# Weight conversions held back to the 40th exponential, the first MLP's share of TensorE started eleven steps late instead of four, and eight PSUM copies moved to ScalarE

## The chip, the cores and the metric

The kernel runs on one core of one Trainium2 chip. The metric is the device time of one execution in microseconds. The time before is the median of three runs, 1116.79 us.

## The reference

The kernel computes three things in a row: an attention with rotary embedding over 4 batches, 8 heads, 576 positions and a head dimension of 64; a first MLP on the 2304 resulting tokens (512 to 2048 to 512), with a piecewise quadratic between its two layers; a second MLP of the same sizes with a squared relu.

```python
def _attn_ref(q, k, v):                       # each (4, 8, 576, 64)
    ...
    q_rot, k_rot = (rotate(q), rotate(k))
    scores = scale * np.matmul(q_rot, k_rot.transpose(0, 1, 3, 2))
    scores = scores - np.max(scores, axis=-1, keepdims=True)
    attn = np.exp(scores)
    attn = attn / (np.sum(attn, axis=-1, keepdims=True) + 1e-09)
    return np.matmul(attn, v).astype(np.float32)

def _moe_ref(x, w_in, w_out):                 # x: (2304, 512)
    h = x @ w_in
    ...
    g = np.where(pos, h, np.where(neg, 0.0, (h + beta) ** 2 / (4.0 * beta)))
    return (g @ w_out).astype(np.float32)

def _moe2_ref(x, w_in, w_out, s, b):
    h = x @ w_in
    r = np.maximum(h, 0.0)
    g = s * (r * r) + b
    return (g @ w_out).astype(np.float32)
```

The MLP weights come as 64-bit floats. Products are made in a reduced 32-bit format on TensorE with each operand split into a high and a low part, so one product is three matmuls (high by high, high by low, low by high).

## The kernel before

**Attention in units.** Two heads make a pair, and there are 16 pairs: four for each batch. A pair is nine units: four blocks of 128 queries for each of its two heads, and one unit for the two heads' last 64 queries together. So there are 144 units, counted from 0, and units 0 to 35 are the first batch. One unit is: scores on TensorE (`sc`, L357), the row maximum on VectorE (`nm`, L359), the exponential on ScalarE (`p`, L364; the list `exps` keeps these instructions, so `exps[n]` is unit n's), four transposes on TensorE (`tp`, L379), a copy of them out of PSUM on ScalarE (L382, L384) or VectorE (L386), and the product with v (`av`, L405). Twice in a pair `trem` transposes what remains of each row, the last 128 columns (`tr`, L392 and L395), and copies it to `ptr` (L397). GpSimd multiplies the next pair's q and k with the rotary table in between (L96 on `qin`, `kin`).

**Weight conversions.** A 128 by 512 block of 64-bit weights is converted in one go: a copy on ScalarE (L134), four bit operations on VectorE (L135 to L138), a rounding copy on ScalarE (L139), then a subtraction and an addition on GpSimd, each in two pieces (L96, tiles `wm` and `w`). Scratch tiles `wa` and `wm` exist once, so conversions follow one another. 24 of them lie inside the attention: 16 blocks of the first MLP's first half (`convert`), and 8 that are written back to memory (`park`).

**The first MLP beside the attention.** When a batch's attention is done, a generator `beside` with that batch's tokens is put on the list `fill`. It is asked for a step some 0.62 times per unit up to unit 76 and 0.92 times later; a step is one block of 12 matmuls (`h` or `y`, L181). Ahead of its first block it yields `LEAD` empty steps. What remains of the list after the last unit is run at the end of the attention. Three such lists come in: 16, 48 and 16 blocks, 960 matmuls together.

**What sets the order.** Up to the end of the attention a list scheduler places each instruction on its engine, by priorities in the order of the code. `tc.issue_after(x)` adds the condition that an instruction isn't issued before x. So `exps[n - 14]` at a conversion is what holds it back. After the attention TensorE's order is that of the code.

Of the kernel before, what the change touches and what calls it, by code (L numbers as in the profile page):

```python
# [24 lines left out]
NP = H // 2  # L25
# [11 lines left out]
RB = 2  # L37
XB = 3
N2 = 464
LEAD = 4  # L40
LT = 2
LA = 4
PB = 3
# [23 lines left out]
def kernel(ctx, tc, qq, kk, vv, tab, ww1, ww2, s, b, out):  # L67
    nc = tc.nc
# [44 lines left out]
    exps, tps, maxs = {}, {}, {}  # L113

    class Slice:
# [6 lines left out]
        def convert(self, raw, pools, hi, lo):  # L122
            if not wide:
                split(hi, lo, raw, nc.scalar, nc.gpsimd)
                return


            top = raw.bitcast(F32).rearrange("p (n t) -> p n t", t=2)[:, :, 1]
            low = raw.bitcast(U16).rearrange("p (n t) -> p n t", t=4)[:, :, 1]
            pool = pools[self.f * 2 + self.made & 1 if len(pools) > 1 else 0]  # L130
            a = pool.tile([P, HW], F32, tag="wa", name="wa", bufs=WB)
            m = pool.tile([P, HW], F32, tag="wm", name="wm", bufs=WB)
            au, mu = a.bitcast(U32), m.bitcast(U32)
            nc.scalar.activation(a, top, AF.Copy, scale=2.0 ** -112)  # L134
            nc.vector.tensor_scalar(out=mu, in0=au, scalar1=3, scalar2=None, op0=ALU.logical_shift_left)  # L135
            nc.vector.scalar_tensor_tensor(out=mu, in0=au, scalar=0x80000000, in1=mu, op0=ALU.bitwise_and, op1=ALU.bitwise_or)
            nc.vector.tensor_scalar(out=au, in0=mu, scalar1=0xFF800000, scalar2=None, op0=ALU.bitwise_and)
            nc.vector.scalar_tensor_tensor(out=a, in0=low, scalar=2.0 ** -36, in1=a, op0=ALU.mult, op1=ALU.mult)  # L138
            nc.scalar.copy(hi, m)  # L139
            pool_tt(out=m, in0=m, in1=hi, op=ALU.subtract)  # L140
            pool_tt(out=lo, in0=m, in1=a, op=ALU.add)
# [108 lines left out]
    def bank(name):  # L250
        return ps_b.tile([P, 512], F32, tag="bank", name=name)
# [6 lines left out]
    def load_qk(i, nm, pieces=WHOLE):  # L258
        bb, hp = divmod(i, NP)
        t = att2.tile([P, 2, S], F32, tag="qkin", name=f"{nm}in", bufs=QB)  # L260
        for c in pieces:
            nc.sync.dma_start(out=t[:, :, c], in_=(qq if nm == "q" else kk)[bb, hp, :, :, c])
        qk_in[nm, i] = t

    def load_v(i):
        bb, hp = divmod(i, NP)
        t = att2.tile([P, 5, 2, D], F32, tag="vin", name="vin", bufs=VB)
        for out, src in ((t[:, :, 1], vv[bb, hp, :, :, 1]), (t[:D, :4, 0], vv[bb, hp, D:, :4, 0]), (t[D:, :4, 0], vv[bb, hp, :D, 1:, 0]), (t[D:, 4, 0], vv[bb, hp, :D, 0, 0])):
            nc.sync.dma_start(out=out, in_=src)
        v_in[i] = t  # L270
# [15 lines left out]
    def rope_pair(i, nm, mul, add, lo_eng, pieces=WHOLE):  # L286

        t = qk_in[nm, i]
        tt = {nc.gpsimd: pool_tt, nc.vector: nc.vector.tensor_tensor}
        last = None  # L290
        for c in pieces:
            tt[mul](out=t[:, :, c], in0=t[:, :, c], in1=tab_sb[:, :, c], op=ALU.mult)
            r = t[:, 1, c]
            tt[add](out=r, in0=t[:, 0, c], in1=r, op=ALU.add)
            last = (lay_q if nm == "q" else lay_k)(i, t, c, lo_eng)
        return last
# [4 lines left out]
    def lay_q(i, t, c, lo_eng, heads=range(2)):  # L301

        st = stacks["q", i] = qs_t[i % 2]
        r = t[:, 1, c]
        for j in heads:
            own, other = SELF[j], SELF[1 - j]
            at = slice(j * QW + c.start, j * QW + c.stop)
            h = nc.scalar.activation(st[own, at], r[own], AF.Copy, scale=0.125)
            m = nc.vector.scalar_tensor_tensor(out=st[other, at], in0=r[own], scalar=0.125, in1=st[own, at], op0=ALU.mult, op1=ALU.subtract)
        return h.ins, m.ins  # L310
# [30 lines left out]
    pt = {}  # L341
# [46 lines left out]
    def trem(i, g):  # L388

        tp = bank("tr")  # L390
        for n in range(2):
            nc.tensor.transpose(tp[:, n * P:(n + 1) * P], p_t.pop((i, 2 * g + n))[:, 512:640], ident)  # L392
        m = 256
        if g == 0:
            nc.tensor.transpose(tp[:, 256:384], p_t.pop((i, 4))[:, 512:640], ident)  # L395
            m = 384
        nc.vector.tensor_copy(pt["r", g][:, :m], tp[:, :m])  # L397

    def av(i, g, ps, kts):

# [63 lines left out]
    def split_x(c, again):  # L464
        xh = m1.tile([P, KD, N1], F32R, tag="xh", name="xh")
        xl = m1.tile([P, KD, N1], F32R, tag="xl", name="xl")
        if again:
            return load_parts((xh, xl), c * N1, N1)
        for k in range(KD):
            xs = m2.tile([P, N1], F32, tag="xs", name="xs", bufs=3)  # L470
            nc.sync.dma_start(out=xs, in_=xd[k, :, c * N1:(c + 1) * N1])
            split(xh[:, k, :], xl[:, k, :], xs, nc.scalar, nc.gpsimd)
        return xh, xl
# [3 lines left out]
    def beside(work):  # L477
        x = split_x(work[0][0], work[0][0] in kept)
        for _ in range(LEAD):
            yield 1.0  # L480
# [48 lines left out]
    def turned_by(t, c):  # L529
        nc.vector.tensor_tensor(out=t[:, :, c], in0=t[:, :, c], in1=tab_sb[:, :, c], op=ALU.mult)  # L530
        return nc.vector.tensor_tensor(out=t[:, 1, c], in0=t[:, 0, c], in1=t[:, 1, c], op=ALU.add).ins
# [53 lines left out]
    def do_load(n):  # L585
        if n == 0:
            with tc.issue_after(turned):
                turned_by(tq, QP[1])
                lay_q(0, tq, QP[1], None)
        elif n in (1, 2):  # L590
            with tc.issue_after(maxs[n]):
                if n == 1:
                    turned_by(tq, QP[2])
                else:
                    lay_q(0, tq, QP[2], None)
        if n < len(units):
            i, k = units[n]
            if i + 1 < NPAIR:
                if i == 0 and k in (2, 6):
                    with tc.issue_after(maxs[k]):  # L600
                        turned_by(qk_in["q", 1], HALVES[k // 6])
                if i == 0 and k in (4, 5, 7, 8):
                    with tc.issue_after(maxs[k]), tc.issue_after(exps[k - 1]):
                        lay_q(1, qk_in["q", 1], HALVES[k // 6], None, [int(k in (5, 8))])
                if i and k == 0:
                    with ExitStack() if i > 1 else tc.issue_after(parts[1][1]), ExitStack() if i > 1 else tc.issue_after(maxs[9]):
                        rope_pair(i + 1, "q", nc.gpsimd, nc.vector, None)
                elif k == 2:
                    with ExitStack() if i else tc.issue_after(exps[2]), ExitStack() if i else tc.issue_after(lowest):
                        rope_pair(i + 1, "k", nc.gpsimd, nc.gpsimd, [nc.gpsimd, nc.vector])  # L610
                elif k == 7:
                    load_v(i + 1)
                elif k in (4, 6) and i + 2 < NPAIR:
                    load_qk(i + 2, "q" if k == 4 else "k")

        if n in range(33, 51, 2) or n in range(70, 110, 4):
            with tc.issue_after(exps[n - 14]):
                convert()

        if n in PARK_AT and parking:  # L620
            with tc.issue_after(exps[n - 4]):
                parking.pop(0).park(wst, scratch)()

    def do_t(n):
        if LT <= n < len(units) + LT:
            i, k = units[n - LT]
            tmain(i, k)
            if k in (4, 8):
                trem(i, k // 8)
                rbs[i, k // 8] = inverse(i, k // 8)  # L630
# [23 lines left out]
    def do_fill(n):  # L654
        if n < 48:
            return
        with tc.issue_after(exps[min(n, len(units)) - 4]):
            run_fill(0.62 if n < 76 else 0.92)

    acts = {"q": do_qk, "l": do_load, "t": do_t, "a": do_av, "f": do_fill}  # L660
    for n in range(len(units) + LA):
        with ExitStack() as st:
# [541 lines left out]
```

## Time and profile before

| | us |
|---|---|
| three runs: median (lowest to highest) | 1116.79 (1115.44 to 1121.0) |
| profiled execution, its own time | 1116.36 |
| its span from the first to the last instruction | 1114.6 |
| TensorE matmul busy | 1071.6 (96%) |
| VectorE busy | 783.8 (70%) |
| ScalarE busy | 626.7 (56%) |
| GpSimd busy | 428.6 (38%) |

Busy time is the union of an engine's instruction times. TensorE's matmuls overlap one another in the records, so its busy time is not the time that its work needs. The granted clock was 0.999 over the span.

### The profile page before, as it was taken

To read this page: it belongs to the slowest core of one execution; us is meant where nothing else is said; L and a number is where in the kernel's file an instruction comes from. 1 tells how busy PE (TensorE), PEld (TensorE's weight loads), DVE (VectorE), ACT (ScalarE), POOL (GpSimd) and SP (SyncE) were. 2 spreads that over 40 slices of the span, in tenths; PEclk is the share of its full clock that TensorE was granted. 3 is DMA by queue.
4 is the path that set the end of the run, shared out by engine and by line. 5 is a ranking of instruction groups with operands and counts; after the bars stand their busy time and mean duration, and the time that the engine had idled before them with its cause. 6 is when DMAs were issued, how large, how long until landed. Compare 5 with 4: busy or idle time off the path is not lost.

```text
span 1114.6 us, 20055 instructions
## 1 busy us (share of the span) xinstructions
PE 1071.6 (96%) x7296; PEld 979.2 (88%) x7296; DVE 783.8 (70%) x1453; ACT 626.7 (56%) x1432; POOL 428.6 (38%) x564
## 2 busy tenths in 40 slices
PE   5898999999999999999999999999999999999998
PEld 4666787778888889999999999999999999999997
DVE  7989998887666663454657666867777778677754
ACT  5777877767656665454545445474555448334431
POOL 6988978785553332332544445110212110000000
PEclk9999999999999999999999999999999999999999
DMA  8665956665656544656465663231322843221220
GB/s 240 170 190 163 270 162 212 216 191 152 213 179 189 173 151 140 223 167 194 146 187 204 211 228 113 94 113 59 116 87 90 303 169 117 83 82 44 81 63 36
DMA packets 109762, 173.24 MB, mean 155 GB/s; under 512 B 29408, under 2 KB 80608, under 8 KB 109664
## 3 DMA queue, kind: packets, MB, share of 16 engines
q1 hardware_dynamic: 109664, 171.97, 49.0%
q8 instruction: 57, 0.93, 0.4%
q14 instruction: 41, 0.34, 0.1%
HBM read 110.10 MB, written 48.56 MB: 142 GB/s over the span
## 4 chain that ended last, share of the span: by engine, by line
PE 73%; DVE 8%; POOL 7%; DMA 6%; ACT 3%; issue 3%; SPq 0%; POOLq 0%; DVEq 0%; ACTq 0%
PE hps L181 14%; PE sum L940 14%; PE yps L856 6%; PE yps L854 6%; PE yps L855 6%; PE yps L790 4%; PE yps L791 4%; PE yps L792 4%; PE h L181 3%; PE sc L357 3%; PE y L181 3%; PE av L405 3%; POOL kin L96 3%; PE tp L379 2%; DVE nm L359 2%
## 5 line engine op out<-in xcount | busy, mean ns | idle before, releaser
L181 PE MATMUL hps<-xh,w 128*128 128x288 f32 (+4 forms) x640 | 163.4, 325 | 0.0
L364 ACT ACTIVATE p<-sc,nm 128x576 f32<-128x576 f32 x144 | 106.5, 741 | 40.6 <-DVE nm L359 35.7
L357 PE MATMUL sc<-kh,qs 128*128 128x288 f32 x336 | 102.6, 328 | 25.6 <-ACT p L364 14.8
L359 DVE TENSOR_REDUCE nm<-sc 128x1 f32<-128x576 f32 x144 | 106.8, 748 | 20.5 <-PE sc L357 19.8
L948 ACT ACTIVATE four<-four,b_sb,s_sb 128x480 f32<-128x480 f32 x64 | 47.4, 782 | 127.8 <-DVE four L947 127.8
L856 PE MATMUL yps<-gh,w 128*128 128x480 f32 (+1 forms) x320 | 118.6, 371 | 0.0
L854 PE MATMUL yps<-gh,w 128*128 128x480 f32 (+1 forms) x320 | 118.5, 370 | 0.0
L855 PE MATMUL yps<-gl,w 128*128 128x480 f32 (+1 forms) x320 | 118.5, 370 | 0.0
L181 PEld LDWEIGHTS hps<-xh,w 128*128 128x128 f32 x640 | 113.3, 188 | 1.0
L96 POOL TENSOR_TENSOR wm<-wm,w 128x256 f32<-128x256 f32 x80 | 67.8, 867 | 109.2 <-ACT w L139 62.3
L181 PE MATMUL hps<-xl,w 128*128 128x288 f32 (+4 forms) x320 | 103.7, 324 | 0.0
L357 PEld LDWEIGHTS sc<-kh,qs 128*128 128x128 f32 x336 | 63.3, 191 | 45.2 <-ACT p L364 26.3
L790 PE MATMUL yps<-gh,w 128*128 128x288 f32 (+3 forms) x288 | 93.2, 323 | 1.2 <-DVE yp L797 0.7
L357 PE MATMUL sc<-kz,qs 128*128 128x288 f32 x336 | 92.9, 299 | 0.0
L792 PE MATMUL yps<-gh,w 128*128 128x288 f32 (+3 forms) x288 | 92.9, 323 | 0.0
L791 PE MATMUL yps<-gl,w 128*128 128x288 f32 (+3 forms) x288 | 92.9, 323 | 0.0
L379 PE MATMUL tp<-ident,p 128*128 128x128 f32 x576 | 87.3, 276 | 2.6 <-DVE pt L386 1.8
L96 POOL TENSOR_TENSOR wm<-wm,raw 128x256 f32<-128x256 f32 x16 | 12.8, 820 | 175.1 <-ACT raw L139 175.1
L405 PE MATMUL av<-pt,vin 128*64 128x256 f32 (+1 forms) x512 | 75.1, 418 | 1.3 <-ACT pt L382 0.8
L181 PE MATMUL y<-gh,w 128*128 128x288 f32 x320 | 73.9, 303 | 1.4 <-ACT pt L382 0.4
L379 PEld LDWEIGHTS tp<-ident,p 128*128 128x128 f32 x576 | 70.1, 142 | 5.6 <-DVE pt L386 2.8
L181 PE MATMUL h<-xh,w 128*128 128x288 f32 x320 | 71.8, 301 | 2.9 <-DVE pt L386 2.1
(153 smaller groups left out, 2888.5 us busy)
## 6 DMA issues: line engine op xcount, KB each, us to landing
wraw<-in_ww SPq DMA_DIRECT2D x56, 512.0 KB, 4.2
w<-parkd SPq DMA_DIRECT2D x24, 512.0 KB, 6.1
kin<-in_k SPq DMA_DIRECT2D x15, 576.0 KB, 5.6
qin<-in_q SPq DMA_DIRECT2D x15, 576.0 KB, 5.1
kh<-kin SPq DMA_DIRECT2D x60, 144.0 KB, 3.1
parkd<-wraw SPq DMA_DIRECT2D x16, 512.0 KB, 3.2
xs<-y1d SPq DMA_DIRECT2D x32, 240.0 KB, 2.7
xd<-u SPq DMA_DIRECT2D x16, 288.0 KB, 2.6
```

The lines of the kernel that those rows point to most:

```text
L96: m = nc.gpsimd.tensor_tensor(out=out[c], in0=in0[c], in1=in1[c], op=op)
L181: m = nc.tensor.matmul(out_ps, l, r, start=(i == 0), stop=(i == n - 1))
L357: nc.tensor.matmul(sc[:, half, o:o + n], l, r[:, k0:k0 + n], start=m == 0, stop=m == len(todo) - 1)
L359: maxs[i * 9 + k] = nc.vector.tensor_reduce(out=nm, in_=sc[:, :, :288], axis=AX.XY, op=ALU.max, negate=True).ins
L379: m = nc.tensor.transpose(v[:, c, :], p[:, c * P:(c + 1) * P], ident)
L790: nc.tensor.matmul(acc, wh, gh, start=f == 0, stop=False)
L791: nc.tensor.matmul(acc, wh, gl, start=False, stop=False)
L792: nc.tensor.matmul(acc, wl, gh, start=False, stop=last)
L854: nc.tensor.matmul(acc, wh, gh, start=f == 0, stop=False)
L855: nc.tensor.matmul(acc, wh, gl, start=False, stop=False)
L856: nc.tensor.matmul(acc, wl, gh, start=False, stop=last)
L940: nc.tensor.matmul(acc, l, r, start=j == 0, stop=j == len(t) - 1)
```

## The change

`LEAD` goes from 4 to 11. The first nine conversions are placed at units 45 to 61 (every second) instead of 33 to 49, and held behind `exps[n - 5]` (units 40 to 56) instead of `exps[n - 14]` (units 19 to 35). In the four pairs of the first batch (`i < NP`) the copy L397 is made by ScalarE instead of VectorE.

```diff
-LEAD = 4
+LEAD = 11
...
-        nc.vector.tensor_copy(pt["r", g][:, :m], tp[:, :m])
+        (nc.scalar.copy if i < NP else nc.vector.tensor_copy)(pt["r", g][:, :m], tp[:, :m])
...
-        if n in range(33, 51, 2) or n in range(70, 110, 4):
-            with tc.issue_after(exps[n - 14]):
+        if n in range(45, 63, 2) or n in range(70, 110, 4):
+            with tc.issue_after(exps[n - 5 if n < 63 else n - 14]):
                 convert()
```

VectorE's row around units 19 to 22, before. `nm` is the maximum of a unit, `pt` and `ptr` are copies out of PSUM, `wm` and `wa` belong to a conversion, `u` is the attention's result.

```order
L386 COPY pt<-tp 128x4x128
L397 COPY ptr<-tr 128x256
L135 TENSOR_SCALAR wm<-wa 128x512
L359 TENSOR_REDUCE nm<-sc 128x1
L136 SCALAR_TENSOR_TENSOR wm<-wa,wm 128x512
L359 TENSOR_REDUCE nm<-sc 128x1
L441 TENSOR_TENSOR u<-av,r 128x256
L443 TENSOR_TENSOR u<-av,r 64x64
L444 TENSOR_TENSOR u<-av,r 64x64
L137 TENSOR_SCALAR wa<-wm 128x512
L386 COPY pt<-tp 128x4x128
L138 SCALAR_TENSOR_TENSOR wa<-wraw,wa 128x512
```

The same place in the changed kernel:

```order
L386 COPY pt<-tp 128x4x128
L359 TENSOR_REDUCE nm<-sc 128x1
L441 TENSOR_TENSOR u<-av,r 128x256
L443 TENSOR_TENSOR u<-av,r 64x64
L444 TENSOR_TENSOR u<-av,r 64x64
L359 TENSOR_REDUCE nm<-sc 128x1
L386 COPY pt<-tp 128x4x128
```

The conversion's four instructions and the copy of `tr` are gone from between the maxima. In ScalarE's row the copy L397 now stands behind an L382 or between two exponentials, and the 24 conversions begin behind exponentials number 41, 45, 51, 57, 62, 67, 70, 75, 79, 81, 85, 88, 90, 96, 100, 106, 108, 111, 115, 117, 119, 123, 129 and 135; before they began behind number 20, 27, 33, 39, 46, 53, 58, 60, 64, 69, 72, 78, 81, 83, 88, 92, 95, 99, 105, 112, 117, 123, 130 and 135.

TensorE's row where the first block of the MLP stands before, around unit 54. `sc` are scores, `tp` transposes, `h` the MLP's first layer.

```order
L435 MATMUL rm<-ident,sume 128x128
L379 MATMUL tp<-ident,p 128x128 x4
L181 MATMUL h<-xh,w 128x288
L181 MATMUL h<-xl,w 128x288
L181 MATMUL h<-xh,w 128x288 x2
L181 MATMUL h<-xl,w 128x288
L181 MATMUL h<-xh,w 128x288 x2
L181 MATMUL h<-xl,w 128x288
L181 MATMUL h<-xh,w 128x288 x2
L181 MATMUL h<-xl,w 128x288
L181 MATMUL h<-xh,w 128x288
L357 MATMUL sc<-kh,qs_107 128x288
```

The same place in the changed kernel:

```order
L435 MATMUL rm<-ident,sume 128x128
L379 MATMUL tp<-ident,p 128x128 x4
L357 MATMUL sc<-kh,qs_107 128x288
L357 MATMUL sc<-kz_109,qs_107 128x288
L357 MATMUL sc<-kh,qs_107 128x288
L357 MATMUL sc<-kz_109,qs_107 128x288
L379 MATMUL tp<-ident,p 128x128 x4
```

The first block moved from behind unit 54's scores to behind unit 66's. In the changed row no MLP matmul stands before that; 336 stand among the scores of units 64 to 111 (before 434), 336 among the last 32 units' (before 288), and 288 behind the last scores (before 168).

TensorE's row a few places behind the last scores (`y` is the MLP's second layer), before:

```order
L433 MATMUL rm<-ident,eb 128x128 x2
L435 MATMUL rm<-ident,sume 128x128
L379 MATMUL tp<-ident,p 128x128 x4
L181 MATMUL y<-gh,w 128x288
L181 MATMUL y<-gl,w 128x288
L181 MATMUL y<-gh,w 128x288 x2
```

and in the changed kernel:

```order
L433 MATMUL rm<-ident,eb 128x128 x2
L435 MATMUL rm<-ident,sume 128x128
L379 MATMUL tp<-ident,p 128x128 x4
L181 MATMUL h<-xh,w 128x288
L181 MATMUL h<-xl,w 128x288
L181 MATMUL h<-xh,w 128x288 x2
```

Both rows fill the end of the attention with MLP blocks. In the changed one the blocks there are earlier ones of the list, and 12 `h` and 12 `y` blocks follow the last scores instead of 6 and 8.

## Rows read from the trace of the kernel before

**Rows 1.** The page: busy time, share of the span, instructions.

```profile
PE 1071.6 (96%) x7296; PEld 979.2 (88%) x7296; DVE 783.8 (70%) x1453; ACT 626.7 (56%) x1432; POOL 428.6 (38%) x564
```

**Rows 2.** Stretches of the attention: us, busy us and instructions of each engine, clock, DMA.

```profile
15.20:41.70 26.50, 21.77 (x139) 16.45 (x140) 25.92 (x40) 18.26 (x44) 23.20 (x30) 1.00 0.69 209
41.70:57.80 16.10, 16.10 (x121) 11.65 (x120) 13.38 (x23) 13.10 (x32) 13.47 (x19) 1.00 0.64 182
57.80:102.30 44.50, 41.09 (x297) 28.70 (x294) 41.36 (x68) 31.76 (x75) 37.40 (x49) 1.00 0.61 180
102.30:164.00 61.70, 56.77 (x433) 45.83 (x432) 56.24 (x93) 48.33 (x117) 56.28 (x74) 1.00 0.69 197
164.00:325.10 161.10, 148.73 (x1143) 129.04 (x1142) 120.59 (x210) 108.21 (x267) 113.61 (x150) 1.00 0.63 196
325.10:417.50 92.40, 91.65 (x719) 82.23 (x718) 60.06 (x115) 63.64 (x162) 29.93 (x48) 1.00 0.57 175
417.50:453.20 35.70, 35.61 (x275) 32.70 (x273) 12.30 (x30) 18.93 (x53) 8.44 (x11) 1.00 0.49 155
```

**Rows 3.** Three of these stretches, the exponential's line alone: two records a unit.

```profile
41.70:57.80 16.10, 6.68 (x17) 1.00 0.64 182
57.80:102.30 44.50, 16.62 (x40) 1.00 0.61 180
...
325.10:417.50 92.40, 24.95 (x63) 1.00 0.57 175
```

**Rows 4.** Busy us and records of MLP matmuls (L181), 440 to 446 us: PE, then PEld.

```profile
440.00:446.00 6.00, 6.00 (x47) 6.00 (x46) 1.00 0.85 275
```

**Rows 5.** The same for three of the stretches of rows 2.

```profile
102.30:164.00 61.70, 12.11 (x76) 10.52 (x77) 1.00 0.69 197
164.00:325.10 161.10, 66.68 (x435) 59.30 (x434) 1.00 0.63 196
325.10:417.50 92.40, 45.90 (x296) 40.25 (x295) 1.00 0.57 175
```

**Rows 6.** Groups by line and shape in 57.8 to 102.3 us.

```profile
L136 DVE SCALAR_TENSOR_TENSOR wm<-wa,wm 128x512 uint32<-128x512 uint32 x4 | 4.0, 1010 | 0.0
...
L138 DVE SCALAR_TENSOR_TENSOR wa<-wraw,wa 128x512 f32<-128x512 uint16 x3 | 3.2, 1065 | 0.0
...
L135 DVE TENSOR_SCALAR wm<-wa 128x512 uint32<-128x512 uint32 x3 | 1.7, 582 | 0.1
L137 DVE TENSOR_SCALAR wa<-wm 128x512 uint32<-128x512 uint32 x4 | 1.7, 428 | 0.0
...
L397 DVE COPY ptr<-tr 128x384 f32<-128x384 f32 x2 | 1.1, 544 | 0.0
...
L438 ACT COPY r<-rm 128x384 f32<-128x384 f32 x2 | 0.9, 474 | 0.0
...
L397 DVE COPY ptr<-tr 128x256 f32<-128x256 f32 x2 | 0.8, 407 | 0.0
```

**Rows 7.** Conversions begun (L134) in three of these stretches: ScalarE busy, count.

```profile
102.30:164.00 61.70, 3.38 (x5) 1.00 0.69 197
164.00:325.10 161.10, 7.39 (x11) 1.00 0.63 196
325.10:417.50 92.40, 2.66 (x4) 1.00 0.57 175
```

**Rows 8.** Waits in 57.8 to 102.3 us: us in total, times, longest.

```profile
ACT p L364 <- DVE nm L359: 7.3, 10, 1.5
POOL qin L96 <- DMA qin<-in_q: 5.2, 2, 3.0
```

**Rows 9.** The chain that ended last in 57.8 to 102.3 us, shares by line.

```profile
by line: issue 17.1%; POOL kin L96 15.3%; DMA kz<-kin 11.5%; POOL qin L96 8.6%; POOL wm L96 7.4%; PE sc L357 6.7%; POOL w L96 5.1%; DVE nm L359 4.3%; PE av L405 3.9%; PE tp L379 3.3%; DMA kin<-in_k 3.2%; DVE wm L136 2.8%; DVE qs L309 2.8%; 
```

**Rows 10.** Steps between an MLP layer's matmuls and the next, 325.1 to 417.5 us.

```profile
L107 DVE TENSOR_TENSOR gl<-h,gh 128x288 fp32r<-128x288 f32 x12 | 5.4, 452 | 1.6 <-ACT gh L103 1.5
...
L103 ACT CAST gh<-h 128x288 fp32r<-128x288 f32 x12 | 4.7, 395 | 1.3 <-DVE h L205 1.3
```

## The prediction

> **What bounds the kernel now.** I read the page's busy times first [rows 1]: TensorE is busy 96% of the span, so whatever the other engines save counts only where TensorE's row becomes shorter. Then the attention cut into stretches [rows 2]. The edges are starts of exponentials: unit 0 starts at 15.2 us, unit 12 at 41.7, unit 20 at 57.8, unit 40 at 102.3, unit 64 at 164.0, unit 112 at 325.1 and unit 143 at 417.5; each unit leaves two records, and one that an edge cuts counts in both stretches [rows 3]. The reader is to see VectorE at 25.92 of 26.5 us in units 0 to 11, 41.36 of 44.5 in units 20 to 39 and 56.24 of 61.7 in units 40 to 63, and only 60.06 of 92.4 in units 112 to 142.
>
> Busy TensorE can't be read as full TensorE here. Where it has nothing but MLP matmuls, 47 records touch 6.00 us [rows 4], two of them cut by the edges, so one costs about 6.00 / 46 = 0.13 us of the row, though the records overlap. In units 112 to 142 TensorE idles 0.75 of 92.4 us [rows 2]. I take that stretch as full: without its 296 MLP matmuls [rows 5], 38.5 us, it leaves 53.9 us for 31 units, or 1.74 us for the attention work of a unit. With these two prices each stretch has a **spare**, which is its time less 1.74 us a unit less 0.13 us a matmul:
>
> - units 12 to 19: 16.1 − 13.9 = 2.2 us, 0.27 a unit, with no conversion but the first one's start (in the order behind exponential 20);
> - units 20 to 39: 44.5 − 34.8 = 9.7 us, 0.49 a unit, with some 3.5 conversions (3 or 4 of each step, [rows 6]);
> - units 40 to 63: 61.7 − 41.8 − 9.9 = 10.0 us, 0.42 a unit, 5 conversions [rows 7], 76 MLP matmuls [rows 5];
> - units 64 to 111: 161.1 − 83.5 − 56.6 = 21.0 us, 0.44 a unit, 11 conversions, 435 matmuls;
> - units 112 to 142: none, by the choice of the price, with 4 conversions.
>
> The work on TensorE is the same before and after. So the change of the time is the change of the spare, summed over the stretches.
>
> By the matmul busy time units 20 to 39 would hold 44.5 − 41.09 = 3.4 us and no more [rows 2]. The Trainium skill, page Perfetto Trace Analysis, section Identifying the Most-Contended Engine, says that this busy time is a poor measure of how near TensorE is to its limit, because matmuls are pipelined, and points to the share of weight loads instead. The trace agrees: weight loads are busy 28.70 of 44.5 us there (64%) against 82.23 of 92.4 in units 112 to 142 (89%) [rows 2]. By the busy time the term for units 20 to 39 below could not pass −3.4 us; by the count it can reach −9.7.
>
> **The change part by part.**
>
> *Copies L397.* Eight copies leave VectorE's row, four of 0.544 us and four of 0.407 us [rows 6]. On ScalarE the nearest row is L438, the same shape out of PSUM: 0.474 us [rows 6]. ScalarE has 18.26 of 26.5 and 31.76 of 44.5 us of work in its stretches [rows 2], and it waits 7.3 us for the maxima in units 20 to 39 [rows 8], so I cost it at nothing. If that cover were gone it would cost up to 8 × 0.474 = 3.8 us. Two of the copies lie in units 0 to 11, where VectorE is nearly full. Bounds 0 and −0.95 us; I take **−0.5**, since the start's chain has loads and GpSimd in it too. The other six count in the next term.
>
> *Units 20 to 39 without conversions.* A conversion's four steps cost VectorE 0.582 + 1.010 + 0.428 + 1.065 = 3.1 us [rows 6]; 3.5 of them are 10.8 of its 41.36 us. Two L96 steps on GpSimd go as well (12.5% of the chain's time there is `wm` and `w`, [rows 9]). What is queued behind: on VectorE the maxima, for which ScalarE's exponential waits, and behind that TensorE's scores. With the conversions gone VectorE needs about 30 us in a stretch that TensorE needs 34.8 us for. What is late next is the rope chain: `kin`, `kz<-kin`, `qin` make up over a third of the chain [rows 9], and GpSimd waits 5.2 us for `qin` to land [rows 8]. Bounds: nothing, and the whole spare, −9.7. The nearest row without conversions is units 12 to 19 at 0.27 a unit: 20 × (0.49 − 0.27) = **−4.3**. This also gives a price for a conversion that has no cover: 4.3 / 3.5 = 1.2 us.
>
> *Units 40 to 63.* Before, 76 MLP matmuls lay here; now none, and 5 conversions begin here as before. It is the picture of the old units 20 to 39 again, with conversions a little denser: 24 × 0.27 + 5 × 1.2 = 12.5 us of spare against 10.0: **+2.5**. The lower bound is 0. The upper one has each conversion cost its whole 3.1 us of VectorE: 6.5 + 15.5 − 10.0 = +12.
>
> *Units 64 to 111.* 13 conversions instead of 11, and 336 MLP matmuls instead of 434. The second list waits its eleven empty steps here (some 12 units), so a part of the stretch has no matmuls to lie beside the conversions. Two more conversions at 1.2 us: **+2.4**. Bounds 0 and 2 × 3.1 = +6.
>
> *Units 112 to 142.* 6 conversions instead of 4; four cost nothing before, GpSimd has 62 us and VectorE 32 us free [rows 2]. Bounds 0 and 2 × 1.2 = +2.4; I take **+1**.
>
> *Behind the last scores.* 288 MLP matmuls instead of 168, in a stretch in which TensorE idled 0.1 us of 35.7 [rows 2]. The work isn't new. What may be lost is the hand-over from a group's last `h` block to its first `y`: a rounding copy and a subtraction, 0.40 + 0.45 us [rows 10], behind three more steps, with the next stage's matmuls to fill. There are two such groups. Bounds 0 and +3; **+0.5**.
>
> *The queues.* SP issues the weight loads of the conversions. The first two are issued early as before and hold their buffers longer; the later ones move behind the first batch's `kin` and `qin` loads. With 0.61 to 0.69 of the DMA engines' time in use [rows 2] I cost this at nothing; a gain in the 5.2 us wait for `qin` is within the bound of units 20 to 39.
>
> **Sum.** −0.5 − 4.3 + 2.5 + 2.4 + 1 + 0.5 = +1.6 us. The profiled execution took 1116.36 us, 0.4 below the median of the three runs. So 1118.0 from its own time and 1118.4 from the median: I say **1118**, no change that can be told. What a measurement of this kernel can tell is about 0.5%, 5.6 us: the three runs lie 5.6 us apart.
>
> **The rivals.**
>
> *Faster: the first batch gains its spare and nothing is given back.* For it: by [rows 2] VectorE and GpSimd are at 41.36 and 37.40 of 44.5 us in units 20 to 39, both are relieved, and units 112 to 142 carry 4 conversions at no spare. Against it: units 12 to 19, with almost no conversions, still have 0.27 a unit. Taken halfway between −4.3 and −9.7, with the whole 0.95 at the start, +1.8 in units 40 to 63 (24 units at the old 0.49 less 10.0) and nothing behind: 1116.4 − 7.0 − 0.95 + 1.8 = 1110. It decides where the spare of units 20 to 39 falls under about 0.16 a unit.
>
> *Slower: units 40 to 63 become VectorE's.* A conversion there has no MLP matmul beside it. If each costs its whole 3.1 us, the stretch has +12: with 1 us for all that follows, 1116.4 − 4.8 + 12 + 1 = 1124.6. It decides at about 2.6 us a conversion: 6.5 + 5 × 2.6 − 10.0 = +9.5, which with −4.8 and +1 is 5.7. For it: VectorE is at 56.24 of 61.7 us there, and its conversions and copies L397 stay. Against it: the measured 1.2 us in units 20 to 39, where there was no MLP either.
>
> *The first batch doesn't gain.* If the rope chain [rows 9] sets its pace and not VectorE, units 20 to 39 give 1 us, the rest stays as above: 1116.4 − 1.5 + 6.4 = 1121.3. This lies at the edge of no change.
>
> **How the numbers follow.** Chances: the sum as written 0.45; no gain in the first batch 0.15; faster 0.21; slower 0.19. The cases of the first two lie within 0.5% of 1116.8 (1111.2 to 1122.4): same 0.60, faster 0.21, slower 0.19. The range leaves out about a tenth on each side and reaches to both outer cases: **1110 to 1125**; the forecast's own is 1114 to 1121.
>
> **What the profile will show.** If the steps are right: units 20 to 39 in about 40 us instead of 44.5, with VectorE under 80% busy; units 40 to 63 in about 54 us, with no MLP matmul; units 64 to 111 some 10 us shorter than 161.1, since 98 matmuls (12.8 us) left and 2.4 us of spare came; some 16 us more of MLP behind the last exponential, TensorE without gaps. Wrong is the step on the first batch if units 20 to 39 take over 43 us or under 38; the step on units 40 to 63 if they take over 58; and the price of a conversion beside MLP work if the spare of units 64 to 142 together moves by more than 6 us. Behind the attention I expect every stage as long as before; a change there would make the whole sum wrong.

## The result and the profile after

The changed kernel takes 1124.87 us (median of 7 runs, 1122.74 to 1128.33) where the kernel before takes 1117.87 us in the 7 runs beside it (1115.44 to 1121.0). The ratio is 1.0076, 95% interval 1.0059 to 1.0092: slower by about three quarters of a per cent (the two medians lie 7.0 us apart, 0.63%). The time lies inside the range, 0.13 us below its upper edge, but the forecast of no change was wrong.

The profiled execution after took 1124.87 us, its span is 1123.1 us, the mean granted clock 0.994 (before 0.999). The page's busy times, which answer to [rows 1]:

```profile
PE 1078.4 (96%) x7296; PEld 985.9 (88%) x7296; DVE 780.2 (69%) x1445; ACT 631.3 (56%) x1440; POOL 428.1 (38%) x564
```

This row says nothing: TensorE is busy 96% again. The same seven stretches, cut at the starts of exponentials 0, 12, 20, 40, 64, 112 and 143, answer to [rows 2]; columns as there (length, busy us and instructions of PE, PEld, DVE, ACT, POOL, then clock, DMA share, GB/s):

```profile
14.40:40.40 26.00, 22.05 (x138) 16.92 (x139) 25.18 (x38) 19.51 (x47) 22.50 (x28) 1.00 0.74 221
40.40:58.60 18.20, 17.57 (x119) 12.29 (x118) 13.60 (x20) 13.07 (x32) 14.05 (x21) 0.91 0.57 155
58.60:99.00 40.40, 40.28 (x295) 28.81 (x294) 30.24 (x50) 29.38 (x73) 26.52 (x39) 1.00 0.58 161
99.00:156.80 57.80, 48.14 (x356) 37.18 (x354) 52.68 (x83) 42.20 (x100) 50.32 (x66) 0.97 0.68 197
156.80:310.10 153.30, 139.77 (x1046) 119.63 (x1046) 124.36 (x213) 106.99 (x263) 118.37 (x154) 0.98 0.63 187
310.10:409.10 99.00, 98.14 (x767) 89.15 (x768) 64.94 (x126) 67.12 (x168) 35.40 (x55) 1.00 0.61 190
```

The last three of these stretches, MLP matmuls alone (PE's busy us and records, clock, DMA share, GB/s), which answer to [rows 5]:

```profile
99.00:156.80 57.80, 0.00 (x0) 0.97 0.68 197
156.80:310.10 153.30, 52.97 (x336) 0.98 0.63 187
310.10:409.10 99.00, 52.85 (x342) 1.00 0.61 190
```

With the prediction's two prices (1.74 us a unit, 0.13 us an MLP matmul) each stretch has again its spare, and the differences add up to the whole:

| stretch | before: us, spare | after: us, spare | change | forecast |
|---|---|---|---|---|
| up to unit 0 | 15.2 | 14.4 | −0.8 | } −0.5 |
| units 0 to 11 | 26.5, 5.6 | 26.0, 5.1 | −0.5 | |
| units 12 to 19 | 16.1, 2.2 | 18.2, 4.3 | +2.1 | none |
| units 20 to 39 | 44.5, 9.7 | 40.4, 5.6 | −4.1 | −4.3 |
| units 40 to 63 | 61.7, 10.0 | 57.8, 16.0 | +6.0 | +2.5 |
| units 64 to 111 | 161.1, 21.0 | 153.3, 26.1 | +5.1 | +2.4 |
| units 112 to 142 | 92.4, 0 | 99.0, 0.6 | +0.6 | +1 |
| from unit 143 on, less 129 moved matmuls at 0.13 us | 697.1 | 714.0 − 16.8 | +0.1 | +0.5 |
| span | 1114.6 | 1123.1 | +8.5 | +1.6 |

The 129 counts five records twice that an edge of the stretches cuts. Behind unit 143's start lie 124 more records of L181 than before (1340 against 1216, those of the second MLP among them); by this count 0.7 us of the change goes from units 64 to 142 to the row behind them.

The first batch gave what was forecast. It was given back more than twice over in units 40 to 111, where both terms came out at more than twice their size.

Matmul busy time would have misled here. In units 20 to 39 it left 3.4 us to gain [rows 2], and 4.1 us were gained, by which TensorE's matmuls are busy for as good as all of the stretch, 40.28 of 40.40 us. Weight loads rose from 28.70 of 44.5 us to 28.81 of 40.40 (64 to 71%) and still show room. In units 40 to 63 they fell from 74 to 64%, in part because 76 MLP matmuls left with their loads, and that is the stretch that lost most. The Trainium skill, page Perfetto Trace Analysis, section Identifying the Most-Contended Engine, says that matmul busy time is not a good measure of how near TensorE is to its limit, because matmuls are pipelined, and names the weight-load share among the measures to use instead. The trace of units 20 to 39 agrees (92% by the first and 64% by the second before, and a tenth of the time was gained).

**What stands in units 40 to 111 now.** The longest waits of TensorE from 40 to 330 us (us in total, times, longest), first after, then before:

```profile
PE sc L357 <- ACT p L364: 16.9, 16, 3.6
```

```profile
PE sc L357 <- ACT p L364: 11.4, 13, 1.8
```

Scores wait for exponentials, which free the buffer that the scores need: half as much again, and the longest wait has doubled. But the cause at the chain's far end is not new. GpSimd's wait for q to land, in the same window, after and then before:

```profile
POOL qin L96 <- DMA qin<-in_q: 18.6, 7, 3.8
```

```profile
POOL qin L96 <- DMA qin<-in_q: 20.5, 7, 5.5
```

GpSimd waits no longer than before. What differs is what TensorE has to do meanwhile. The longest wait after, around 140 us, in the timeline (start, length, engine, instruction, in brackets the idle time ahead and what ended it):

```profile
136.20 0.76 DVE L359 TENSOR_REDUCE nm<-sc 128x1 f32<-128x576 f32 x1 [0.16 <-PE sc L357]
...
138.47 3.83 POOL L96 TENSOR_TENSOR qin<-qin,tab_sb 128x288 f32<-128x288 f32 x4 [2.84 <-DMA qin<-in_q]
...
139.71 1.17 DVE L138 SCALAR_TENSOR_TENSOR wa<-wraw,wa 128x512 f32<-128x512 uint16 x1
...
142.34 1.33 DVE L294 TENSOR_TENSOR qin<-qin 128x576 f32<-128x576 f32 x1 [1.45 <-POOL qin L96]
...
143.93 1.40 DVE L359 TENSOR_REDUCE nm<-sc 128x1 f32<-128x576 f32 x2
...
144.70 0.74 ACT L364 ACTIVATE p<-sc,nm 128x576 f32<-128x576 f32 x1 [3.11 <-DVE nm L359]
...
145.58 0.40 PE L357 MATMUL sc<-kh,qs 128*128 128x288 f32 x1 [3.64 <-ACT p L364]
```

Read from the bottom: the scores wait 3.64 us for an exponential, that one 3.11 us for its maximum, and the maximum stands in VectorE's row behind a conversion's four steps (L135 to L138, of which the last is shown) and behind L294, the rope's addition, which itself waits 1.45 us for GpSimd, which waited 2.84 us for q. Between two maxima lie 7.7 us (136.20 to 143.93). Now the place around 140 us before, where a conversion and L294 stand between two maxima as well:

```profile
139.49 0.76 DVE L359 TENSOR_REDUCE nm<-sc 128x1 f32<-128x576 f32 x1 [0.63 <-PE sc L357]
...
140.76 1.24 DVE L294 TENSOR_TENSOR qin<-qin 128x576 f32<-128x576 f32 x1
...
143.30 0.38 PE L181 MATMUL h<-xh,w 128*128 128x288 f32 x1
...
144.84 0.29 PE L181 MATMUL h<-xh,w 128*128 128x288 f32 x1
...
145.13 1.18 DVE L138 SCALAR_TENSOR_TENSOR wa<-wraw,wa 128x512 f32<-128x512 uint16 x1
146.23 0.74 DVE L359 TENSOR_REDUCE nm<-sc 128x1 f32<-128x576 f32 x1
```

The maxima are 6.7 us apart (139.49 to 146.23), and TensorE does not stand still: up to 143.30 us the attention's own matmuls run, then a block of MLP matmuls, and TensorE is busy all of the time from 140 to 150 us. After, no MLP matmul stands there until 158.6 us. The block takes some 1.7 us and the wait after is 3.64 us, so these two places alone don't show that the block would have covered it.

**The clock.** Four of TensorE's stretches ran partly at its lower level (1.2 instead of 2.4 GHz, 0.5 in the column's measure, so a figure between is a mixture). The windows after, columns as above:

```profile
40.00:46.00 6.00, 6.00 (x35) 4.20 (x35) 3.09 (x6) 3.24 (x9) 6.00 (x10) 0.72 0.50 149
140.00:150.00 10.00, 6.36 (x40) 6.09 (x40) 6.88 (x11) 5.44 (x13) 9.86 (x15) 0.84 0.37 113
202.00:208.00 6.00, 4.41 (x20) 3.92 (x21) 4.19 (x7) 4.08 (x11) 5.57 (x7) 0.74 0.91 264
250.00:256.00 6.00, 3.57 (x16) 3.54 (x17) 4.28 (x8) 3.51 (x9) 5.86 (x10) 0.72 0.22 69
```

Before, all four windows stand at 1.00. Ahead of the second and the last fall TensorE had just idled, 3.64 us up to 145.58 and 2.59 us up to 252.43, both in the chain told above. Ahead of the first it had idled 1.86 us up to 39.76; but before it idled 1.66 us at the same place, up to 41.02, and no fall came. Ahead of the third no wait was longer than 0.9 us. The first fall lies in units 12 to 19 (+2.1 us), for which the prediction had no term.

### The profile page after: what moved, and what is told of

Same layout as the page of the kernel before. It is cut to its first block, busy times and chain, and to the rows that moved or that the text cites. A ratio compares the mean times of both kernels' runs of the same rounds, so it can differ in the third digit from the quotient of the medians.

```text
span 1123.1 us, 20085 instructions
## 1 busy us (share of the span) xinstructions
PE 1078.4 (96%) x7296; PEld 985.9 (88%) x7296; DVE 780.2 (69%) x1445; ACT 631.3 (56%) x1440; POOL 428.1 (38%) x564
## 4 chain that ended last, share of the span: by engine, by line
PE 77%; DMA 6%; DVE 6%; POOL 5%; issue 2%; ACT 2%; SPq 1%; POOLq 0%; ACTq 0%; DVEq 0%
PE hps L181 14%; PE sum L940 13%; PE yps L856 6%; PE yps L854 6%; PE yps L855 6%; PE y L181 5%; PE sc L357 4%; PE h L181 4%; PE yps L790 4%; PE yps L791 4%; PE yps L792 4%; PE av L405 3%; PE tp L379 3%; POOL kin L96 2%; DVE nm L359 1%
## 5 line engine op out<-in xcount | busy, mean ns | idle before, releaser
L181 PE MATMUL hps<-xh,w 128*128 128x288 f32 (+4 forms) x640 | 163.8, 325 | 0.0
L357 PE MATMUL sc<-kh,qs 128*128 128x288 f32 x336 | 105.8, 336 | 30.0 <-ACT p L364 20.2
L96 POOL TENSOR_TENSOR wm<-wm,w 128x256 f32<-128x256 f32 x80 | 72.1, 921 | 114.5 <-ACT w L139 72.6
L181 PEld LDWEIGHTS hps<-xh,w 128*128 128x128 f32 x640 | 113.4, 188 | 1.0
L181 PE MATMUL hps<-xl,w 128*128 128x288 f32 (+4 forms) x320 | 103.7, 324 | 0.0
L357 PE MATMUL sc<-kz,qs 128*128 128x288 f32 x336 | 95.3, 304 | 0.0
L379 PE MATMUL tp<-ident,p 128*128 128x128 f32 x576 | 89.3, 281 | 4.8 <-DVE u L441 1.2
L379 PEld LDWEIGHTS tp<-ident,p 128*128 128x128 f32 x576 | 72.5, 145 | 6.9 <-DVE pt L386 1.6
L181 PE MATMUL y<-gh,w 128*128 128x288 f32 x320 | 72.5, 300 | 1.5 <-ACT ys L507 0.8
L107 DVE TENSOR_TENSOR gl<-hps,gh 128x288 fp32r<-128x288 f32 (+4 forms) x88 | 46.4, 527 | 39.3 <-ACT gh L103 39.1
```

The costliest lines, as they stand in the source:

```text
L181: m = nc.tensor.matmul(out_ps, l, r, start=(i == 0), stop=(i == n - 1))
L357: nc.tensor.matmul(sc[:, half, o:o + n], l, r[:, k0:k0 + n], start=m == 0, stop=m == len(todo) - 1)
L379: m = nc.tensor.transpose(v[:, c, :], p[:, c * P:(c + 1) * P], ident)
```

## The experiments

In each, "before" is the kernel before in runs beside it, whose medians are 1116.4 to 1117.4 us. Spare is worked out as above, from the times between the same exponentials and the records of L181. Kernels are named by these short names below. What theories A and B are is told in the first expectation.

**The parts, one by one.** *Only the copies on ScalarE:*

```diff
-        nc.vector.tensor_copy(pt["r", g][:, :m], tp[:, :m])
+        (nc.scalar.copy if i < NP else nc.vector.tensor_copy)(pt["r", g][:, :m], tp[:, :m])
```

> Only the eight copies L397 of the first batch move to ScalarE; conversions and LEAD as before. Theory A (the MLP's late start leaves TensorE without blocks to lie over the waits of units 54 to 66 and 88 to 97, it stands still there and is granted the lower clock behind it): no change, 1116 to 1119 us. Theory B (the conversions behind the 40th exponential cost VectorE's time where nothing hides them): the same. If the copies themselves delay ScalarE's exponentials: over 1121 us, with a fall of the clock near 41 us as in the changed kernel.

Measured: 1112.6 us, ratio 0.9968 (0.9954 to 0.9983). This one line alone makes the kernel faster, by 4.8 us between the medians (1.9 to 5.1 us by the interval). Neither theory had forecast that. Its units 20 to 39 (row 1), 40 to 63 and 64 to 111:

```profile
56.10:97.80 41.70, 40.47 (x297) 28.98 (x295) 35.75 (x61) 31.87 (x77) 36.36 (x48) 1.00 0.65 191
97.80:158.60 60.80, 56.08 (x420) 44.52 (x419) 54.55 (x92) 47.11 (x115) 55.64 (x73) 1.00 0.66 194
158.60:320.10 161.50, 153.17 (x1162) 133.05 (x1161) 121.37 (x215) 111.44 (x272) 114.11 (x153) 0.99 0.65 198
```

Units 20 to 39 go from 44.5 to 41.7 us, with conversions still in them, but about one fewer: 2 begin there instead of 3, and of the 5.6 us that VectorE has less to do, the copies make up 1.9 and conversion steps 3.2. The stretches behind are as before to within 1 us.

*Only the conversions later, LEAD 4:*

```diff
-        if n in range(33, 51, 2) or n in range(70, 110, 4):
-            with tc.issue_after(exps[n - 14]):
+        if n in range(45, 63, 2) or n in range(70, 110, 4):
+            with tc.issue_after(exps[n - 5 if n < 63 else n - 14]):
```

> Only the conversions move behind the 40th exponential; LEAD 4 and the copies on VectorE as before. The first MLP block again stands behind unit 54's scores. Theory A: the first batch keeps its gain of some 4 us and the holes are gone, 1113 to 1118 us, clock 0.998 or more. Theory B: 1121 to 1126 us, since the conversions are as packed as in the changed kernel (nine of them between exponentials 63 and 81).

Measured: 1133.89 us, ratio 1.0145 (1.0126 to 1.0164). TensorE's waits from 40 to 330 us:

```profile
PE y L181 <- POOL w L96: 10.7, 6, 3.2
PE sc L357 <- ACT p L364: 7.5, 11, 2.1
PE y L181 <- ACT w L139: 3.0, 2, 1.7
```

The MLP's second layer waits 13.7 us for weights that are converted too late. Units 20 to 39 take 40.6 us, units 64 to 111 take 181.3. Both theories had forecast less.

*Only LEAD:*

```diff
-LEAD = 4
+LEAD = 11
```

> Only LEAD goes from 4 to 11; conversions from the 20th exponential on and the copies on VectorE as before. The first MLP block stands behind unit 65's scores. Theory A: 1120 to 1126 us, TensorE waits of over 2 us in units 54 to 66 or 88 to 97 and a clock under 0.998. Theory B: 1116 to 1119 us, since the conversions stand as before.

Measured: 1123.54 us, ratio 1.0049 (1.003 to 1.0068): some 6 us slower by a number that takes no work away and adds none. In units 40 to 63, without MLP matmuls, the spare is 12.8 us (before 10.0), in units 112 to 142 1.8. Its units 12 to 19 take 17.6 us at a granted clock of 0.91. Every engine's order is that of the kernel before up to 132.9 us, so this fall of the clock, in after as here, needs nothing that the change did.

*The changed kernel with `LEAD = 4`:*

```diff
-LEAD = 11
+LEAD = 4
```

> The changed kernel with LEAD 4: conversions behind the 40th exponential and copies on ScalarE stay. Theory A: 1112 to 1118 us, units 20 to 39 near 40 us as in the changed kernel, clock 0.998 or more. Theory B: 1121 to 1126 us, as the changed kernel.

Measured: 1134.53 us, ratio 1.0169 (1.0147 to 1.0191). TensorE's waits from 40 to 330 us:

```profile
PE sc L357 <- ACT p L364: 9.2, 13, 1.7
PE y L181 <- POOL w L96: 8.1, 5, 2.2
PE y L181 <- ACT w L139: 3.5, 3, 1.7
```

Again both theories had forecast less. So late conversions and a late MLP are a pair: on top of the copies alone (1112.6 us) the late conversions cost 21.9 us, and LEAD 11 gives back 9.7 of it.

**Is it the late MLP, the conversions, or the clock?** *Copies and LEAD 11, conversions where they were before:*

```diff
-LEAD = 4
+LEAD = 11
...
-        nc.vector.tensor_copy(pt["r", g][:, :m], tp[:, :m])
+        (nc.scalar.copy if i < NP else nc.vector.tensor_copy)(pt["r", g][:, :m], tp[:, :m])
```

> The copies on ScalarE and LEAD 11, conversions as before. If the parts add up: 1117.4 less 4.8 (copies) plus 6.2 (LEAD alone) is 1118.8; the late conversions then cost the other 6 us of the changed kernel (1124.9). If the late conversions cost nothing once LEAD is 11 (their cost was the waits of y blocks for weights, which LEAD 11 takes away): 1123 to 1126, as the changed kernel.

Measured: 1126.88 us, ratio 1.0078 (1.0059 to 1.0097). That is no better than the changed kernel: with LEAD 11 the late conversions cost nothing more. And it is 14.3 us slower than the copies alone, from which it differs in one number. Not all of this is LEAD's doing: between the profiled executions lie 15.3 us, and 4.8 of them lie ahead of the first instruction in which the two orders differ (a matmul at 129.2 us there and 134.1 us here), 2.7 of them in units 12 to 19, whose clock is 0.92 here and 1.00 there. The lowest runs of the two are 12.2 us apart. Its units 40 to 63, 64 to 111 and 112 to 142:

```profile
102.10:158.50 56.40, 49.63 (x359) 36.87 (x358) 49.85 (x83) 41.86 (x98) 50.54 (x68) 0.97 0.69 197
158.50:309.60 151.10, 137.06 (x1029) 119.24 (x1029) 119.68 (x204) 105.22 (x259) 112.91 (x148) 0.97 0.61 187
309.60:411.10 101.50, 100.17 (x787) 90.06 (x782) 63.54 (x123) 65.14 (x166) 32.24 (x51) 1.00 0.57 176
```

Against the copies alone the spare is +4.7 us, +3.8 and +3.1 in these three, and in the first two the clock is 0.97 where it was 1.00 and 0.99. Were all of TensorE's slow time on the path, the clock would make up 1.7 of the 4.7 us and some 3 of the 3.8.

From the first instruction that differs to the start of unit 64, copies alone and then this kernel:

```profile
129.20:158.60 29.40, 27.43 (x209) 23.42 (x208) 25.61 (x47) 22.11 (x56) 24.71 (x33) 1.00 0.55 163
134.10:158.50 24.40, 20.57 (x147) 15.71 (x146) 20.84 (x38) 16.84 (x39) 19.17 (x27) 0.93 0.60 170
```

The first has 70 MLP matmuls, 9.1 us at 0.13, and the second none; yet it is only 5.0 us shorter. So 4.1 us of spare came with their leaving, and TensorE's scores wait 3.8 us for exponentials instead of 0.7. The same cut between the kernel before (132.9 to 164.0 us, 76 matmuls) and LEAD 11 alone (133.4 to 158.8 us, none) gives 4.2 us. At most 1.7 to 1.8 us of either is the clock's, which is 0.93 in both of the kernels with LEAD 11.

*Matmuls that nobody reads, in the thin units:* four matmuls of 128x224 each behind the scores of 36 of the units 8 to 12, 50 to 65, 74 to 79 and 86 to 97, into a part of the scores' buffer that isn't used.

```diff
+THIN = {*range(8, 13), *range(50, 66), *range(74, 80), *range(86, 98)}
...
+        if j is not None and i * 9 + k in THIN:
+            for _ in range(4):
+                nc.tensor.matmul(sc[:, 1, 288:512], l, r[:, :224], start=True, stop=True)
```

> The changed kernel with four more matmuls of 224 columns, whose result nobody reads, behind the scores in units 8 to 12, 50 to 65, 74 to 79 and 86 to 97 (not in each pair's unit 4): some 35 times 0.4 us, 14 us more for TensorE, where it stood still. Theory A, with the lower clock as the carrier: the clock rises to 0.998 or more and the time stays or falls, 1118 to 1125 us. If the clock is no cause and TensorE's spare was no spare: 1128 to 1139 us. If the spare takes the matmuls but the clock gives nothing back: 1124 to 1128.

Measured: 1139.73 us, ratio 1.0187 (1.0162 to 1.0212), 14.9 us above the changed kernel and above all three ranges, 0.10 us for each of the 144 by division; but units 20 to 39, which have none of them, take 2.3 us longer too. As a filler they are no fair test: they write the scores' buffer, and the unit's own maximum waits for them. VectorE's wait from 40 to 330 us (here L363 is the maximum and L361 the added matmul):

```profile
DVE nm L363 <- PE sc L361: 9.4, 10, 3.2
```

They didn't hold the clock up either: its mean is 0.994 as without them, and units 40 to 63 show 0.94. Since it didn't rise, this kernel can't tell what the clock costs.

*The changed kernel without two of VectorE's four conversion steps* (L136 and L137 are left out inside the attention, so the weights are others):

```diff
+    light = [1]
...
-            nc.vector.scalar_tensor_tensor(out=mu, in0=au, scalar=0x80000000, in1=mu, op0=ALU.bitwise_and, op1=ALU.bitwise_or)
-            nc.vector.tensor_scalar(out=au, in0=mu, scalar1=0xFF800000, scalar2=None, op0=ALU.bitwise_and)
+            if not light:
+                nc.vector.scalar_tensor_tensor(out=mu, in0=au, scalar=0x80000000, in1=mu, op0=ALU.bitwise_and, op1=ALU.bitwise_or)
+                nc.vector.tensor_scalar(out=au, in0=mu, scalar1=0xFF800000, scalar2=None, op0=ALU.bitwise_and)
...
+    light.clear()
```

> The changed kernel with two of the four VectorE steps (L136, L137) left out of the conversions inside the attention, so the weights made there are wrong; ScalarE, GpSimd and the DMAs do the same as before. It takes 24 times 1.5 us from VectorE in units 40 to 135. Theory B (the conversions' VectorE time in units 40 to 111 is what costs): 1116 to 1121 us. Theory A: 1122 to 1126 us, since the waits come from the loads of q and the missing MLP blocks.

Measured: 1116.95 us, ratio 0.9993 (0.9981 to 1.0006), 7.9 us below the changed kernel. *The same two steps left out of the kernel before:*

> The kernel before with L136 and L137 left out of the conversions inside the attention (wrong weights), as was done to the changed kernel, where it gave 8 us. If MLP blocks cover what the conversions cost VectorE from unit 54 on, units 64 to 111 gain less here than the 8.8 us of the changed kernel's profile, 1 to 4 us, and units 20 to 39 some 3 us: 1110 to 1114 us in all. If the cover makes no difference: 1105 to 1109 us.

Measured: 1114.98 us, ratio 0.9989 (0.998 to 0.9998), 1.4 us below before, just above the range expected for a cover. This isn't what the steps are worth: in its profiled execution units 0 to 19, ahead of the first step that is left out, take 47.1 us instead of 42.6, units 12 to 19 at a clock of 0.87. Units 40 to 63 and 64 to 111, of the first and then of the second kernel:

```profile
99.60:156.00 56.40, 48.33 (x360) 37.56 (x358) 45.38 (x77) 41.98 (x100) 50.63 (x70) 0.97 0.71 203
156.00:297.70 141.70, 132.10 (x1027) 115.65 (x1027) 106.96 (x185) 106.65 (x262) 115.19 (x156) 0.99 0.67 208
```

```profile
102.30:160.90 58.60, 53.66 (x412) 43.36 (x411) 48.01 (x82) 47.11 (x117) 53.10 (x73) 1.00 0.70 203
160.90:323.50 162.60, 153.67 (x1168) 135.55 (x1167) 105.57 (x189) 109.94 (x269) 107.12 (x150) 0.98 0.64 195
```

In units 64 to 111 VectorE is relieved of 17.4 us in the one and 15.0 us in the other. The changed kernel's spare there falls by 11.6 us (26.1 to 14.5), that of the kernel before by 0.2 (21.0 to 20.8; 448 MLP records lie in it instead of 435). In units 40 to 63 of the changed kernel 7.3 us off VectorE bring 1.4. Two more things differ in units 64 to 111. GpSimd waits 34.9 us for q in the kernel before without the steps and 15.3 with them; in the changed kernel it waits 5.0 and 11.4. And the clock goes from 1.00 to 0.98 in the kernel before, which can hide some 3 us of a gain, and from 0.98 to 0.99 in the changed one, which can give some 2.

*LEAD 11 for the first list of MLP blocks only:*

```diff
-        for _ in range(LEAD):
+        for _ in range(LEAD if work is ORDERS[0] else 4):
```

> The changed kernel with LEAD 11 for the first list alone; the second and third list wait four empty steps as before, so units 88 to 97 have MLP blocks again. Theory A: the falls of the clock behind unit 88 are gone and units 64 to 111 lose some 4 us less: 1119 to 1122 us. If the cost lies in units 40 to 66 alone: 1124 to 1126 us.

Measured: 1122.29 us, ratio 1.0039 (1.0023 to 1.0055), 2.6 us below the changed kernel and just above theory A's range; the profiled execution, at 1126.12 us, is the slowest of its eight. Units 64 to 111 hold 420 MLP records instead of 336 and have 20.3 us of spare instead of 26.1; units 112 to 142 take 3.4 of that back.

**How much does an earlier MLP cover?** The copies on ScalarE, with `LEAD = 7` and `LEAD = 2`:

> Conversions as before, copies on ScalarE, LEAD 7: the first MLP block stands behind unit 60's scores (54 with LEAD 4, 65 with LEAD 11). If the late start itself is the price, by the units that lack MLP blocks: between 1112.6 (LEAD 4) and 1126.9 (LEAD 11), 1117 to 1122 us. If LEAD 11 is one bad order of the scheduler and the start doesn't matter: 1111 to 1115 us.

> The same with LEAD 2: the first block behind unit 52's scores, 96 MLP matmuls left behind the last scores instead of 168. If MLP blocks earlier in the attention cover its waits: 1109 to 1112 us. If the blocks then wait for their weights, as with LEAD 4 and the late conversions: over 1116 us, with waits of y for GpSimd's w.

Measured: 1124.29 us, ratio 1.0076 (1.0053 to 1.0098), and 1120.53 us, 1.0032 (1.002 to 1.0044). LEAD 7 is above the range expected for a late start. With the two kernels above this gives a row by the same line of code (time in us, MLP records, spare in us):

| copies on ScalarE, with | units 40 to 63 | units 64 to 111 |
|---|---|---|
| LEAD 2 | 57.8, 75, 6.3 | 174.0, 477, 28.5 |
| LEAD 4 (copies alone) | 60.8, 70, 9.9 | 161.5, 445, 20.1 |
| LEAD 7 | 58.8, 36, 12.4 | 157.9, 396, 22.9 |
| LEAD 11 | 56.4, 0, 14.6 | 151.1, 336, 23.9 |

In units 40 to 63 the spare rises as the MLP records go, though not in step with them: from LEAD 2 to 4 it rises by 3.6 us for 5 records. Cut where the order first differs from that of the copies alone, the stretch up to unit 64 takes, without its MLP matmuls at 0.13 us, 20.3 us with 70 of them (LEAD 4), 22.8 with 36 (LEAD 7, 133.1 to 160.6 us, clock 0.94) and 24.4 with none (LEAD 11). In units 64 to 111 LEAD 2 breaks the row, by waits of another kind (100 to 330 us):

```profile
PE y L181 <- DVE gl L107: 6.3, 2, 5.2
```

The second layer of a block waits for its own first layer's result: asked for too early, the MLP becomes a wait itself. The waits expected, for GpSimd's `w`, are not the ones that came.

**Copies on ScalarE for two batches** (`i < 2 * NP`):

> The copies L397 of the first two batches on ScalarE, all else as before. If it is VectorE's time that counts wherever it is nearly full: 1108 to 1112 us (copies of the first batch alone: 1112.6). If ScalarE has no room beside the MLP blocks of the second batch: 1113 to 1117 us.

Measured: 1118.81 us, ratio 1.0017 (1.0003 to 1.003), 6.2 us worse than for one batch. Units 40 to 63 take 62.5 and 64 to 111 167.5 us (60.8 and 161.5 with one). GpSimd's wait for q is 29.5 us between 100 and 330 us, against 8.6 with one batch: from 103 us on, where the first copy of the second batch moved, the list scheduler lays out every engine's row anew. Both ranges were missed, and why this kernel is slower is not shown.

## Why the prediction was wrong

**The step that failed** is the term of units 40 to 63, "It is the picture of the old units 20 to 39 again", and under it the sentence "The work on TensorE is the same before and after". The first MLP was counted as work that takes 0.13 us a matmul wherever it stands, and moving some of it behind the attention (124 matmuls by the trace) as free. LEAD had no term of its own. But beside the attention these matmuls fill the time in which scores wait for VectorE, and behind the attention there is nothing to fill. LEAD 11 alone costs 6 us, and 14 us on top of the copies, of which about a third lies ahead of the first instruction that it moves. From that instruction to unit 64 the time beside the MLP matmuls rises by 4.1 us on top of the copies and by 4.2 alone, and by 2.5 where half of the matmuls stay. So some 4 of the +6.0 us in units 40 to 63 come with the blocks' leaving, up to 1.7 of them by way of the lower clock; the rest of the +6.0 is not explained. The timelines around 140 us show one such place: a gap of some 7 us between maxima, with TensorE busy before and idle for 3.64 us after.

**The price of a conversion**, 1.2 us wherever it stands, carries the second term that failed. The forecast for units 64 to 111 was +2.4 for two more conversions, and +5.1 came. The two kernels with half the VectorE steps fit the same reading: with MLP blocks in most units, 15 us less of VectorE's work there brought 0.2 us of spare, and with blocks missing in units 54 to 66 and 88 to 97, 17 us less brought 11.6. But GpSimd's wait for q rose by 19.6 us in the one and fell by 6.4 in the other. What is measured is that the term came out at more than twice its size; that the price depends on the cover is a reading which the late loads of q leave open. Of the +5.1 us itself some 3 can be the clock's (0.98 instead of 1.00).

**Units 20 to 39** came as forecast, −4.1 against −4.3, VectorE 75% busy. But the parts don't add up as I wrote them: the copies alone give −2.8, the conversions alone −3.9, both −4.1. The conversions' move bought little on top of the copies; since about one conversion had left these units with the copies as well, how their −2.8 splits is open. The copies' own term, up to unit 11, was −0.5 and came out at −1.3; but 0.8 of that lies ahead of unit 0, whose start varies between kernels by more than that without the copies (14.2 to 15.5 us), so −0.5 is what units 0 to 11 show. On ScalarE they cost what L438 suggested [rows 6]:

```profile
L397 ACT COPY ptr<-tr 128x384 f32<-128x384 f32 x2 | 1.0, 486 | 0.0
...
L397 ACT COPY ptr<-tr 128x256 f32<-128x256 f32 x2 | 0.7, 367 | 0.2 <-PE tr L392 0.2
```

**Right were** the counts of conversions, which answer to [rows 7] (5, 13 and 6 as forecast), the term of units 112 to 142, and the end: +0.1 where +0.5 was forecast. Behind the last `y` of the attention, at 461.2 us, lie 661.9 us (before, behind 453.1, 661.5).

```profile
99.00:156.80 57.80, 3.41 (x5) 0.97 0.68 197
156.80:310.10 153.30, 8.80 (x13) 0.98 0.63 187
310.10:409.10 99.00, 4.02 (x6) 1.00 0.61 190
```

**The rivals.** The slower one gave 1124.6 us, and the time is 1124.87; that is luck, for its mechanism is not what happened. It wanted +12 us in units 40 to 63 with VectorE as the bound; +6.0 came, and with 7.3 us taken off VectorE that stretch hardly shortened. The faster one needed less than 0.16 us of spare a unit in units 20 to 39; they kept 0.28. The bound on units 40 to 63 that I set as the sign of a wrong step, 58 us, was just not reached (57.8), because I had set it for a larger loss; the 54 us forecast was missed by 3.8. The sign set for the price of a conversion, 6 us of spare in units 64 to 142, was just not reached either (+5.7).

**The clock's part.** In the profiled executions the mean clock differs by 0.005 of the span, so at most some 5.6 us of the 8.5 could be its doing, if all of TensorE's slow time were on the path. Over the runs the median clock is 0.997 before and 0.994 after. Runs at 0.997 took 1115.03 to 1120.54 us before (10 runs) and 1122.74 to 1124.02 after (3 runs), so most of the loss is there at an equal clock too. By stretches of the profiled execution the slow time is at most 1.7 of the +2.1 us in units 12 to 19, 1.7 of the +6.0 in units 40 to 63, and some 3 of the +5.1 in units 64 to 111.

**What stays open.** In units 40 to 63 some 2 of the +6.0 us are left beside the missing blocks, and VectorE's steps bring 1.4 there; GpSimd, 50.32 of 57.8 us busy and late with q, is the nearest to it that no run took apart. How much of the differences of a few us between these kernels comes from the scheduler's new order, and not from the part that was edited, can't be told by them. Why the clock fell near 41 us in some kernels' runs and not in others' with the same order is open as well.

The best version found is the copies alone: 1112.6 us, ratio 0.9968 (0.9954 to 0.9983) to the kernel before.

## What to carry to other kernels

Work that a busy engine does between steps of a chain is not neutral ballast: it covers the chain's waits, so moving it has a price even where its own time is unchanged. Before moving it, look in the trace at what would stand open without it, here the longest gap between two maxima in VectorE's row. And try the parts of a change alone: one of three was worth 5 us, and the other two were a pair of which one gave back less than half of what the other cost (9.7 of 21.9 us). Where a list scheduler sets the order, compare two kernels from the first instruction that differs: a third of a difference of 15 us lay ahead of it here.

## What was not expected of the hardware

The granted clock went to its lower level in dense-looking work, behind a wait of 1.86 us: 0.72 from 40 to 46 us after, with matmuls busy 6.00 of 6.00 us by the records, while the kernel with the same order of that stretch as before (LEAD 11 alone) showed it too and the kernel before did not in its profile. Matmul records stretch when that happens: a transpose (L379) takes 354 ns on the mean from 40 to 46 us and 272 ns from 46 to 56 us, so matmul busy time reads full where TensorE only works more slowly. And 144 unread matmuls in the thin units neither kept the clock up nor came free.
